# A 2048-token mixer on one core: first weights of the 64-channel unit centered on TensorE, and a new order of loads and steps

## The chip, the cores and the metric

One NeuronCore of a Trainium2 chip runs the whole program. The metric is the time of one execution on the device in microseconds, as the median of several runs. The profile is that of one execution. In it PE is TensorE's matmuls, PEld its weight loads, DVE is VectorE, ACT ScalarE, POOL GpSimd, and SP the engine that issues most DMAs.

## What is computed

For 2048 tokens x of 448 channels, the result is `g * a + (1 - g) * b`, with a sigmoid gate g per token. Branch a is a state-space convolution, which the kernel replaces by running sums wherever a check on the parameters allows. Branch b is what this case is about:

```python
h  = gelu(layernorm(x) @ w1)                     # 448 -> 448
hs = concat(h[:, 0:112] shifted +1 token, h[:, 112:224] shifted -1,
            h[:, 224:336] shifted +2, h[:, 336:448] shifted -2) @ w2
x1 = x + hs
b  = x1 + gelu(layernorm(x1) @ w3) @ w4          # 448 -> 1792 -> 448
```

## The kernel before

Tokens go in four blocks of 512, and each block runs two layers. A "unit" is a tile of at most 128 hidden channels: per block four units of the mixing layer (groups 0, 2, 1, 3 in this order, so unit numbers 0, 1, 2, 3 of block 0 and 4, 5 of block 1 are groups 0, 2, 1, 3 and 0, 2), then 14 units of the second layer. Group 2 has only 64 channels of its own; this is the "64-channel unit" (unit number 1). Each unit takes a first product (x times w1, function `first`), a GELU on ScalarE, and a second product into four accumulators (`second`).

Products are made in split precision. Each operand is cut into a high part and a low part, by a ScalarE copy into the reduced type and a VectorE subtraction, and high x high, low x high and high x low are summed. The 448 rows of x stand in four chunks of 128 partitions (index k); the last chunk has only 64 rows, and its upper half holds the low part.

The mean of the layer norm is taken out of the weights: w1 loses its column means before the split ("centering"), so that x need not be centered. The means come from TensorE: a matmul whose stationary operand is a column of 1/448 repeated 128 times (`cm`) leaves in each of the 128 rows of a PSUM bank the column means of w1; VectorE then subtracts them (`center`). These matmuls are full fp32, two instructions each; the products use the reduced type, one instruction each.

All of the first 35 us is issued in an order written by hand, the string ORDER (L1090). Each word is one step, and steps of an engine run in the order of the string:

- `w` a warming matmul; `m0` to `m3` the column means of group 0 to 3 (L912, L927, L863); `wt`, `ws` VectorE sums of chunks, so that m2 and m0 need fewer matmuls; `c0` to `c3` centering on VectorE (L935); `h0` to `h3` the high part on ScalarE and `l0` to `l3` the low part on VectorE of a group's first weights; `wh`, `wl` the same for its second weights
- `xha`, `xhb`, `xla`, `xlb` high and low parts of the left and right half of x's first block; `xh1`, `xl1` of the second block
- `p1:h2a` a first product of unit 1 with the high weights, chunk 2 (x in place of h: low part of x; l: low weights), on the left half a, on b, or on all 512 tokens; `s0:12` a second product of unit 0
- `sa`, `sb` token statistics, `ra0` nine small VectorE steps to 1/sqrt(variance), `ra`, `rm`, `rn` its rows, turned by TensorE; `xz`, `pe`, `sk` the first tokens of the shifted groups: `pe` (L839) multiplies the centered weights of groups 1 and 3 by two tokens
- `mu`, `hd`, `cp`, `tl` scaling, GELU, high and low part of a unit's hidden values

The loads of this stage are issued in `first_loads` (L255), most by SP and three by ScalarE. A DMA waits for the completion slot of an earlier one before it is issued. The names used below: u0a, u0b (two halves of group 0's w1), u1, u2, u3 (w1 of the other groups), xa, xb, xc (left half of x's first block, chunks 0-1 and 2-3, and its right half), t0 to t5 tokens for the statistics, v0, v1 the second weights, n1 the next block, id the identity matrix. In this order two steps of ScalarE's queue stand ahead of its first arithmetic, and SP issues xa first.

Of the kernel before, what the change touches and what calls it, by code (L numbers as in the profile page):

```python
# [179 lines left out]
def mixer_and_small_steps(ctx, tc, xs, gg, okm, x, xT, xb, x0, w1, w2, w3, w4, gate, par, logdt, dskip, ident, out):  # L180
# [74 lines left out]
    def first_loads():  # L255

        r = raw[0] = room([128, 4 * XW], "raw")
        parts0.append(r[:, :4 * HW].rearrange("p (k t) -> p k t", k=4))
# [7 lines left out]
        load_w1(act, 2)
        sp(r[:, :2 * HW], x0[:, :2 * HW])
        act(w1r[:, :256], w1[:, :256])  # L268
        sp(w1r[:, 256:512], w1[:, 256:512])
        act(xs[:, 0, :], x[0:128])  # L270
        sp(r[:, 2 * HW:4 * HW], x0[:, 2 * HW:4 * HW])
        load_w1(sp, 1)
        load_x(1, 2)
        load_x(2, 3)
        load_w1(sp, 3)
        load_x(3, 5)
        sp(r[:, 4 * HW:], x0[:, 4 * HW:])
        sp(idt, ident)
        sp(w2r[:, 0], w2[:, 0])  # L279
        load_xt(1)  # L280
        sp(w2r[:, 1:4], w2[:, 1:4])
        load_x(NT + 1, 2 * NT + 1)
# [621 lines left out]

    WS = {}

    def presum():

        WS[1] = big.tile([128, 128], F32, name="ws", tag="lt")
        nc.vector.tensor_add(WS[1], W1R[0][:, 0, :], W1R[0][:, 1, :])  # L910

    def presum_mean():  # L912
        a, p = W1R[0], mean_bank(0)
        for q, (c, r) in enumerate(((1, a[:, 3, :]), (0, a[:, 2, :]), (0, WS[1]))):
            nc.tensor.matmul(p, cm[:, c:c + 1].to_broadcast([128, 128]), r, start=q == 0, stop=q == 2)

    def presum_unit2():

        a = W1R[2]
        v = big.tile([128, GD], F32, name="ws", tag="yt")  # L920
        WS[0] = v
        nc.vector.tensor_add(v, a[:, 0, :], a[:, 1, :])
        yield
        nc.vector.tensor_add(v, v, a[:, 2, :])
        yield

    def unit2_mean():  # L927

        p = mean_bank(2)
        for q, c in enumerate((1, 0)):  # L930
            nc.tensor.matmul(p, cm[:, c:c + 1].to_broadcast([128, 128]), WS[0] if q else W1R[2][:, 3, :],
                             start=q == 0, stop=q == 1)
            yield
# [160 lines left out]
    p2:l2a p0:h0b p3:h2a xlb p2:h0a sa1 p1:h1b p2:x2a p3:h3a p2:h1b sb3 p0:h2b xlb p0:l0b sa2 p2:h0b p1:x0b
    xlb p3:x1b p0:x2b,h1b l3 p0:l1b p2:x0b wh0 p1:x2b p0:x0b p1:h3b ra0 p0:x1b ra0 p0:h3b p2:x2b ra0 p3:h1b
    xh1 p3:l3a ra0 p3:x2b p2:l0a ra0 p2:l0b ra0 xh1 p1:h0b p3:h2b ra0 p3:l2b p2:x1b ra0 p0:l3b xh1 ra0
    p2:h3b p1:x1b sk p1:h2b wl0 p0:l2b xh1 p3:l1a ra sk uf0 sk p2:l2b xl1 rm p2:l1a p3:x0b uf1 p3:l0b mu0
    p3:x0a sk p4:l1 mu0 p4:h1 sk ad1 p2:h2b hd0 p3:l3b,h0b p4:h3 hd0 mu0 p3:l2a mu1 p2:l1b bm p2:l3a mu1
    p3:h3b hd0 p3:x1a,h1a,l1b hd0 p4:l2 xl1 s0:00 hd0 s0:10 p5:h3 xl1 hd0 p4:x0 s0:01 ba p5:h0 sb7 s0:20 hd0
    hd1 p2:l3b tl0 s0:21 p3:l0a p5:x1 sb7 wh2 mu2 s0:30 p5:x0 cp1 p4:h2 sb5 p3:h0a s0:02 wh1 p4:h0 tl0 s0:11  # L1100
    sb5 s0:31 tl1 hd2 s0:22 p5:h2 p4:l3 wl2 hd2 p5:h1 hd2 s0:12 sb7 p4:x1 cp2 s1:11,31 sb5 s1:20 cp2 s1:01
    sb7 s0:32 sb5 s2:30 tl2 s1:30,10 s2:20 ra1 mu3 s2:00 s1:21 s2:22 ra1 s1:00 wl1 hd3 p4:l0 s2:10 ra1 wh3
    s2:02 ra1 s2:01 ra1 s2:31 hd3 xl1 hd3 s2:11,32,21 ra1 cp3 s2:12 ra1 p4:x2 ra1 wl3 p5:x2 s3:30 uf5 s3:20
# [198 lines left out]
```

## Time and profile before

| | before |
|---|---|
| median of 3 runs | 371.17 us (371.15 to 371.31) |
| the profiled execution, first to last instruction | 368.9 us |
| TensorE busy | 363.4 us (99%) |
| VectorE / ScalarE / GpSimd busy | 84% / 59% / 17% |

The page gives busy time of each engine, the chain of work that ended last, and the costliest groups of instructions. A line of a timeline is: start, duration, engine, source line, operation, output and inputs, shape, count of merged instructions. Matmuls overlap at their ends, so the distance between two starts is what one costs, and its duration is longer.

### The profile page before, as it was taken

The page shows a single profiled execution, that of the slowest core. Times are in us where ns is not written, and L with a number is a line of the kernel's source. Part 1 is how long each engine was busy: PE and PEld are TensorE (multiplying, and loading weights), DVE is VectorE, ACT ScalarE, POOL GpSimd, SP SyncE. Part 2 cuts the span into 40 slices and gives each one's busy share as a digit, 9 for nine tenths or more (in the row PEclk, how much of TensorE's full clock was granted, in tenths as well). Part 3 has the DMA queues.
Part 4 walks back from the last instruction along what each step waited for, and adds up shares of the span by engine and source line. Part 5 has one row for each costly group of instructions (what it writes and reads, how often), then busy time and mean ns, then how long its engine had stood idle before and what let it go on. Part 6 is the DMA issues. An engine that isn't in the chain of part 4 may idle for free.

```text
span 368.9 us, 5308 instructions
## 1 busy us (share of the span) xinstructions
PE 363.4 (99%) x1734; PEld 314.3 (85%) x1734; DVE 308.1 (84%) x571; ACT 215.9 (59%) x383; POOL 63.3 (17%) x176
## 2 busy tenths in 40 slices
PE   8999999999999999999999999999999999999995
PEld 4988888888888888888888888888888888888885
DVE  4999979797999997378799899998789999998533
ACT  5987668777684637944274774554756645455220
POOL 1000432000300000110013433224243234000000
PEclk9999999999999999999999999999999999999999
DMA  7994116626948064001833514457385611361213
GB/s 258 393 398 157 38 65 124 134 88 251 390 134 203 0 116 156 0 0 52 178 107 77 89 28 94 114 165 131 83 131 121 179 16 28 79 179 30 64 50 105
DMA packets 88479, 46.14 MB, mean 125 GB/s; under 512 B 67200, under 2 KB 82944, under 8 KB 87808
## 3 DMA queue, kind: packets, MB, share of 16 engines
q1 hardware_dynamic: 88016, 45.27, 45.6%
q10 hardware_dynamic: 432, 0.49, 0.4%
q8 instruction: 15, 0.25, 0.3%
q14 instruction: 16, 0.13, 0.1%
HBM read 34.74 MB, written 11.01 MB: 124 GB/s over the span
## 4 chain that ended last, share of the span: by engine, by line
PE 93%; DMA 4%; ACT 1%; DVE 0%; ACTq 0%; SPq 0%; issue 0%
PE p L478 46%; PE acc L603 45%; DMA raw<-xb_in 2%; DMA xs<-x_in 2%; PE acc L638 1%; ACT xh L394 1%; PE p L638 0%; PE misc L363 0%; DVE xh L401 0%; ACT uf L996 0%; ACTq L268 0%; DVE uf L1007 0%; SPq L279 0%; ACT ug L1020 0%; ACT ug L1023 0%
## 5 line engine op out<-in xcount | busy, mean ns | idle before, releaser
L539 ACT ACTIVATE uf<-p 128x512 f32<-128x512 f32 x56 | 33.4, 597 | 113.3 <-PE p L478 113.2
L478 PE MATMUL p<-xh,w3l 128*128 128x512 f32 x224 | 70.1, 394 | 0.0
L478 PE MATMUL p<-xh,w3h 128*128 128x512 f32 x224 | 70.1, 394 | 0.0
L758 DVE TENSOR_TENSOR_SCAN z<-z,carry 128x512 f32<-128x512 f32 x48 | 61.5, 1282 | 4.2 <-POOL z L752 0.5
L603 PE MATMUL acc<-w4l,uh 128*128 128x448 f32 x216 | 56.3, 367 | 0.0
L603 PE MATMUL acc<-w4h,uh 128*128 128x448 f32 x216 | 56.0, 365 | 0.0
L603 PE MATMUL acc<-w4h,ul 128*128 128x448 f32 x216 | 55.8, 364 | 0.0
L569 DVE TENSOR_TENSOR ul<-uf,uh 128x512 fp32r<-128x512 f32 x56 | 38.1, 681 | 20.1 <-ACT uh L549 20.0
L478 PEld LDWEIGHTS p<-xh,w3l 128*128 128x128 f32 x224 | 42.1, 188 | 9.8
L478 PE MATMUL p<-xl,w3h 128*128 128x512 f32 x168 | 47.7, 392 | 0.0
L478 PEld LDWEIGHTS p<-xh,w3h 128*128 128x128 f32 x224 | 42.1, 188 | 6.6
L603 PEld LDWEIGHTS acc<-w4h,uh 128*128 128x128 f32 x216 | 40.5, 188 | 6.0
L603 PEld LDWEIGHTS acc<-w4h,ul 128*128 128x128 f32 x216 | 40.6, 188 | 3.5
L603 PEld LDWEIGHTS acc<-w4l,uh 128*128 128x128 f32 x216 | 40.6, 188 | 3.4
L753 ACT ACTIVATE z<-zs,nu 128x512 f32<-128x512 f32 x64 | 42.3, 710 | 0.6 <-DMA zs<-xT_in 0.6
L478 PEld LDWEIGHTS p<-xl,w3h 128*128 128x128 f32 x168 | 31.5, 188 | 7.2
L549 ACT ACTIVATE uh<-uf 128x512 fp32r<-128x512 f32 x56 | 35.4, 633 | 1.8
L752 POOL COPY z<-carry 128x1 f32<-128x1 f32 x48 | 32.1, 679 | 16.0 <-DVE zs L764 15.9
L760 POOL COPY carry<-z 128x1 f32<-128x1 f32 x48 | 13.1, 273 | 105.7 <-DVE z L758 105.0
L344 POOL TENSOR_TENSOR t<-r 128x4 f32<-128x4 f32 (+1 forms) x5 | 3.1, 627 | 117.4 <-DVE r L343 117.4
L603 PE MATMUL acc<-w2l,uh 128*128 128x448 f32 x64 | 19.9, 368 | 0.0
L758 DVE TENSOR_TENSOR_SCAN z<-z,carry,zero 128x512 f32<-128x512 f32 x16 | 19.9, 1247 | 0.0
(207 smaller groups left out, 541.8 us busy)
## 6 DMA issues: line engine op xcount, KB each, us to landing
zs<-xT_in SPq DMA_DIRECT2D x4, 1024.0 KB, 8.3
yd<-yt SPq DMA_DIRECT2D x56, 64.0 KB, 2.0
ysb<-yd SPq DMA_DIRECT2D x16, 224.0 KB, 2.7
raw<-xb_in SPq DMA_DIRECT2D x3, 1032.0 KB, 12.6
raw<-w_in SPq DMA_DIRECT2D x3, 1024.0 KB, 5.6
xd<-xt SPq DMA_DIRECT2D x16, 192.0 KB, 2.1
xr<-xd SPq DMA_DIRECT2D x16, 192.0 KB, 3.1
raw<-w_in SPq DMA_DIRECT2D x3, 896.0 KB, 4.6
```

Source lines behind the costliest of these rows:

```text
L344: eng.tensor_mul(t, y, y)
L394: nc.scalar.activation(XH["a", b][:, k, :], raw[b][:, k, :], AF.Copy)
L478: nc.tensor.matmul(p[:, t0:t1], (wl if w else wh)[:, k, :], (xl if x_ else xh)[:, k, o + t0:o + t1], start=(q == 0 and fresh), stop=stop i ...
L539: nc.scalar.activation(UF[n], P1[n], AF.Gelu_apprx_tanh)
L549: nc.scalar.activation(UH[n], UF[n], AF.Copy)
L569: nc.vector.tensor_sub(UL[n], uf, f32(UH[n]))
L603: nc.tensor.matmul(ACC[j], (UL if p == 2 else UH)[n][:, t], wl if p == 1 else wh, start=first_, stop=last_)
L638: nc.tensor.matmul(acc, (UL if p == 2 else UH)[m][:, t], (wl if p == 1 else wh)[:, c], start=q == last and m == n and p == 0, stop=m > n a ...
L752: nc.gpsimd.tensor_copy(z4[:, m, 0:1], carry[:, k, m:m + 1])
L753: nc.scalar.activation(z4[:, m, 1:], ZS[b][:, k, :], AF.Copy, scale=nu[:, k, m:m + 1])
L758: nc.vector.tensor_tensor_scan(z, z, up, carry[:, k, m:m + 1], OP.add, OP.add)
L760: nc.gpsimd.tensor_copy(carry[:, k, m:m + 1], z[:, TB - 1:])
```

## The change

The 64-channel unit: its four chunks (4 x 64 columns) are no longer summed on VectorE and centered there. TensorE computes the centered weights in PSUM: four full-precision matmuls put minus the mean into all 256 columns, and a fifth, with the identity matrix, adds the weights. The split into high and low part reads PSUM. Group 0's means take four matmuls, with no sum on VectorE. Groups 1 and 3 get their means in one accumulation of four matmuls of 256 columns (`mean_ops(1, 3)`). The first block of x lies in DRAM as three contiguous pieces. The loads follow a list: first all of w1 and the tokens t0, then the identity matrix, then x. The order of steps is a new one.

```diff
-    cm = big.tile([128, 2], F32, name="cm")
+    cm = big.tile([128, 4], F32, name="cm")
...
+        def x0_part(q):
+            w = (2 * HW, 2 * HW, 4 * (XW - HW))
+            return x0[sum(w[:q]) * 128:sum(w[:q + 1]) * 128].rearrange("(p t) -> p t", p=128)
...
+        for word in LOADS.split():
+            queue, _, job = word.partition(":")
+            jobs[job](act if queue == "act" else sp)
...
+        for c, s in ((2, -1.0), (0, 1.0)):
+            nc.gpsimd.memset(cm[:, c:c + 1], s / D)
+            nc.gpsimd.memset(cm[:64, c + 1:c + 2], s / D)
+            nc.gpsimd.memset(cm[64:, c + 1:c + 2], 0.0)
...
-        pm[g] = ps.tile([128, GD if g == 2 else 128], F32, name="pm", tag=("misc", "acc2", "acc1", "acc3")[g], bufs=1)
-        return pm[g]
+    def mean_bank(gs):
+        g = gs[0]
+        p = ps.tile([128, len(gs), GD if g == 2 else 128], F32, name="pm", tag=("misc", "acc1", "acc2")[g], bufs=1)
+        for q, g in enumerate(gs):
+            pm[g] = p[:, q, :]
+        return p
...
+    def mean_ops(*gs):
+        p = mean_bank(gs)
         for k in range(4):
             c = int(k == 3)
-            nc.tensor.matmul(p, cm[:, c:c + 1].to_broadcast([128, 128]), W1R[g][:, k, :], start=k == 0, stop=k == 3)
+            w = W1R[gs[0]] if len(gs) == 1 else w1r[:, W1O[1]:].rearrange("p (i k m) -> p k i m", i=2, k=4)
+            nc.tensor.matmul(p, cm[:, c:c + 1].to_broadcast([128, 128]), w[:, k], start=k == 0, stop=k == 3)
+            yield
+
+    def centered_ops(g):
+        w = W1R[g]
+        p = pm[g] = ps.tile(list(w.shape), F32, name="pm", tag=("misc", "acc1", "acc2")[g], bufs=1)
+        for k in range(4):
+            c = 2 + int(k == 3)
+            nc.tensor.matmul(p, cm[:, c:c + 1].to_broadcast([128, 128]), w[:, k:k + 1, :].to_broadcast(list(w.shape)),
+                             start=k == 0, stop=False)
+            yield
+        nc.tensor.matmul(p, idt, w, start=False, stop=True)
+        yield
...
-            return w1d[:, k0:k1, :GD], w1d[:, k0:k1, GD:], W1R[g][:, k0:k1]
+            return w1d[:, k0:k1, :GD], w1d[:, k0:k1, GD:], pm[g][:, k0:k1]
...
-    TASKS.update(wt=presum_unit2(), m2=unit2_mean(), c2=each((center, 2, 0, 2), (center, 2, 2, 4)),
+    TASKS.update(m0=mean_ops(0), m1=mean_ops(1, 3), m2=centered_ops(2),
...
+    LOADS = """
+    sp:u0b sp:u2 act:u0a act:t0 sp:u1 sp:u3 act:id sp:xa sp:xb sp:xc sp:t1 sp:t3 sp:t2 sp:n1 sp:v1 sp:v0 sp:t5
+    """
+
...
-    w w wt xha w wt m2 w xla m2 ws c2 m0 c2 h2 h2 l2 l2 p1:h0a c0 xha xz p1:x0a sk w xz sa0 xla p1:h2a m1 c0
-    h0 xla sa1 l0 p0:x0a p1:x1a p0:h0a c1 p1:x2a h0 p1:h1a,h3a sa0 ld m3 l0 h1 p0:h3a c3 p0:x2a,l2a,l1a sa2
...
+    w sa0 w w m0 xz m0 m0 m0 c0 h0 m2 c0 h0 sa0 m2 m2 sk m2 w m2 h2 h2 w xha l0 l0 m1 m1 m1 l2 l2 m1 c3 p1:h1a
+    p0:l1a c1 xla p1:h0a p0:h0a xz p0:l0a,h1a xha xla xla pe p1:h2a p0:h2a ld p0:l2a h1 p2:h1a h3 p0:x0a,x1a l1
+    p2:h2a p1:x1a p2:h0a p1:x2a p2:x2a xhb xhb p0:h3a,h0b p1:x0a p0:l0b p2:h1b p0:l3a p1:h3a sa1 p1:h2b
...
```

## Rows read from the trace of the kernel before

**Rows 1.** The page: span, and busy time, share and instructions by engine.
```profile
span 368.9 us, 5308 instructions
...
PE 363.4 (99%) x1734; PEld 314.3 (85%) x1734; DVE 308.1 (84%) x571; ACT 215.9 (59%) x383; POOL 63.3 (17%) x176
```
**Rows 2.** The chain in order of time: start us, us, what.
```profile
21.02 0.67 PE acc L603 x2
...
360.04 3.68 PE acc L638 x18
```
**Rows 3.** Stretches: us, busy PE, PEld, DVE, ACT, POOL (count); clock, DMA, GB/s.
```profile
0.00:4.56 4.56, 3.62 (x10) 1.27 (x11) 0.11 (x1) 1.83 (x3) 0.90 (x15) 1.00 0.54 165
4.56:10.57 6.01, 5.24 (x37) 4.41 (x38) 4.96 (x15) 4.21 (x13) 0.45 (x3) 1.00 1.04 360
...
21.02:34.20 13.18, 13.18 (x66) 11.67 (x67) 12.83 (x34) 9.51 (x23) 0.00 (x0) 1.00 0.78 285
...
10.86:28.58 17.72, 17.64 (x122) 16.05 (x121) 17.15 (x48) 14.39 (x34) 0.90 (x4) 1.00 1.02 394
```
**Rows 4.** Timeline of PE up to 35 us.
```profile
0.77 3.62 PE L903 MATMUL pw<-const-bfloat16-1.0 128*128 128x512 bf16 x10 [0.77 <-PEq L1294]
4.56 0.41 PE L931 MATMUL pm<-w1r,cm 128*128 128x64 f32 x2 [0.17 <-DMA w1r<-w_in]
4.80 0.38 PE L903 MATMUL pw<-const-bfloat16-1.0 128*128 128x512 bf16 x1
...
5.26 0.66 PE L915 MATMUL pm<-w1r,cm 128*128 128x128 f32 x4
...
6.71 0.39 PE L478 MATMUL p<-xh,w1d 128*128 128x256 f32 x1 [0.38 <-DVE w1d L943]
...
7.85 0.39 PE L478 MATMUL p<-xh,w1d 128*128 128x256 f32 x1 [0.40 <-ACT xh L956]
8.07 1.05 PE L867 MATMUL pm<-w1r,cm 128*128 128x128 f32 x8
...
9.08 0.28 PE L478 MATMUL p<-xl,w1d 128*128 128x256 f32 x1
...
9.67 1.15 PE L867 MATMUL pm<-w1r,cm 128*128 128x128 f32 x8
10.57 0.36 PE L478 MATMUL p<-xh,w1h 128*128 128x256 f32 x1
...
20.43 0.52 PE L478 MATMUL p<-xh,w1l 128*128 128x256 f32 x2
...
21.53 0.39 PE L478 MATMUL p<-xh,w1d 128*128 128x512 f32 x1
...
34.15 0.85 PE L478 MATMUL p<-xh,w1h 128*128 128x512 f32 x3
```
**Rows 5.** Two lines' matmuls: ns min/median/max, first and last start.
```profile
L867 PE MATMUL pm<-w1r,cm x16: 272/275/363, 8.1 to 10.5; 128*128 128x128 f32 x16
...
L845 PE MATMUL pe<-w1r,xz x8: 191/193/194, 12.2 to 12.4; 128*2 128x32 f32 x8
```
**Rows 6.** Timeline of DVE: c3, the step after it, and wl1.
```profile
10.86 0.69 DVE L937 TENSOR_TENSOR w1r<-w1r,pm 128x512 f32<-128x512 f32 x1 [0.42 <-PE pm L867]
11.46 0.62 DVE L974 BATCH_NORM_STATS2 b<-xs 128x6 f32<-128x448 f32 x1
...
28.58 0.62 DVE L943 TENSOR_TENSOR w2l<-w2r,w2h 128x448 fp32r<-128x448 f32 x1
```
**Rows 7.** SP's own waits, 0 to 20 us: total, times, longest.
```profile
SPq L246 <- DMA w1r<-w_in: 1.4, 1, 1.4
SPq L278 <- DMA xs<-x_in: 0.9, 1, 0.9
```
**Rows 8.** Line L267 (xa): from issue to landing.
```profile
DMA to landing us min/median/max: 3.5/3.5/3.5
```
**Rows 9.** Line L264 (u2 by ACT; u1, u3 by SP): from issue to landing.
```profile
DMA to landing us min/median/max: 3.7/4.8/5.7
```

More of the change, by code (lines that the diff above doesn't have):

```diff
@@ L264, in load_w1, with load_to @@
             queue(w1r[:, t], w1[:, t])
[L266 to L282, printed above, removed]
+        def load_to(queue, j0, j1):
+            queue(xs[:, j0:j1, :], x[j0 * 128:j1 * 128].rearrange("(j p) d -> p j d", p=128))
+        jobs = dict(
+            u2=lambda q: load_w1(q, 2), u1=lambda q: load_w1(q, 1), u3=lambda q: load_w1(q, 3),
+            u0a=lambda q: q(w1r[:, :256], w1[:, :256]), u0b=lambda q: q(w1r[:, 256:512], w1[:, 256:512]),
+            xa=lambda q: q(r[:, :2 * HW], x0_part(0)), xb=lambda q: q(r[:, 2 * HW:4 * HW], x0_part(1)),
+            xc=lambda q: q(r[:, 4 * HW:], x0_part(2)),
+            t0=lambda q: load_to(q, 0, 1), t1=lambda q: load_to(q, 1, 2), t2=lambda q: load_to(q, 2, 3),
+            t3=lambda q: load_to(q, 3, 5), t5=lambda q: load_to(q, NT + 1, 2 * NT + 1),
+            id=lambda q: q(idt, ident), v0=lambda q: q(w2r[:, 0], w2[:, 0]), v1=lambda q: q(w2r[:, 1:4], w2[:, 1:4]),
+            n1=lambda q: load_xt(1))
+        for word in LOADS.split():
+            queue, _, job = word.partition(":")
+            jobs[job](act if queue == "act" else sp)
     def constants():
-        nc.gpsimd.memset(cm[:, 0:1], 1.0 / D)
-        nc.gpsimd.memset(cm[:64, 1:2], 1.0 / D)
-        nc.gpsimd.memset(cm[64:, 1:2], 0.0)
+        for c, s in ((2, -1.0), (0, 1.0)):
+            nc.gpsimd.memset(cm[:, c:c + 1], s / D)
+            nc.gpsimd.memset(cm[:64, c + 1:c + 2], s / D)
+            nc.gpsimd.memset(cm[64:, c + 1:c + 2], 0.0)
         nc.gpsimd.memset(one, 1.0)
@@ L903, in warm_up @@
             nc.tensor.matmul(pw, warm[:, 0:128], warm, start=True, stop=True)
[L905 to L933, printed above, removed]
     def center(g, k0=0, k1=4):
@@ L1051, in mixer_and_small_steps @@
     TASKS = dict(
-        ws=each((presum,)), m0=each((presum_mean,)), w=each(*((warm_up, 1) for _ in range(5))),
+        w=each(*((warm_up, 1) for _ in range(5))),
         xha=each((x_hi, 0, lh), (x_hi, 2, lh)), xhb=each((x_hi, 0, rh), (x_hi, 2, rh)),
@@ L1073, in mixer_and_small_steps @@
         if g:
-            TASKS[f"m{g}"] = each((col_means, g))
             TASKS[f"c{g}"] = each((center, g))
@@ L1094, in mixer_and_small_steps @@
[L1094 to L1103, printed above, removed]
@@ new lines, in mixer_and_small_steps @@
+    sb3 p2:l0a l3 sb3 sa2 sb3 sa2 p2:l2a p1:x0b p3:x1a,h3a p2:x0a xlb p0:h3b p1:h3b p3:l2b uf1 xh1 p0:l2b,l3b
+    uf0 p2:x2b,h3b,l3a p3:h0b sb3 ra0 ra0 ra0 p3:l0b ra0 p2:x1b ra0 ra0 p2:l1b ra0 p3:l3a ra0 p2:h2b ra0 p3:h2b
+    p2:l1a p3:h1a ad1 sk ra mu0 mu0 rm mu1 p3:l1b p2:l3b,l2b xh1 xh1 p5:h0 mu1 p4:h0 p3:l3b p4:l0 mu0 xh1 p4:h1
+    p3:x1b hd0 wh0 xl1 xl1 hd0 wl0 hd0 hd0 ba hd0 hd1 p3:l2a,h0a p4:h2 sk xl1 p5:h1 p2:x1a,l0b hd0 p3:x0b hd0
+    xl1 p3:h2a p5:h3 s0:10 p3:x2b sb5 p3:x0a p4:x0,l1 bm p3:x2a tl0 p3:l0a,l1a tl0 p4:x1 mu2 p5:x0 cp1 sb5 p5:x1
@@ new lines, in mixer_and_small_steps @@
+    wh1 s0:00 tl1 p4:l3 wh2 hd2 p3:h3b p4:h3,l2 p5:x2,h2 s0:22 wl2 sk sk s0:32 sb7 s0:01,31 sk s1:00 hd2 s0:11
+    hd2 cp2 s0:21 s1:01 p4:x2 s1:20 s0:12 s1:11 mu3 sb7 s1:21 s0:30,02 s1:10 s0:20 s1:31 tl2 s2:32,30,22 hd3 wh3
+    sb7 sb5 s2:10 sb7 s2:02 sb5 wl1 cp2 ra1 s2:12 hd3 hd3 cp3 s1:30 s2:31 ra1 wl3 s2:21,00 ra1 cp3 s2:20 s3:20
+    s2:01 ra1 uf5 ra1 s3:00 ra1 s3:21 ra1 s3:11 s2:11 ra1 ra1 rn tl3 s3:01 sb9 s3:32,31,12,10 sb9 bn mu4 hd4 hd4
+    s3:02 re re s3:22 re ad5 s3:30 hd4 cp4 tl4 cp4 re mu5 hd5 cp5
@@ L1278 @@
         x=x, xT=xT, xb=np.stack([xT[:, :, b * TB:b * TB + XW] for b in range(1, NB)]),
-        x0=np.concatenate([xT[:, :, t].reshape(128, -1) for t in (slice(0, HW), slice(HW, XW))], axis=1),
+        x0=np.concatenate([xT[:, k, t].ravel() for k, t in ((slice(0, 2), slice(0, HW)), (slice(2, 4), slice(0, HW)),
+                                                            (slice(0, 4), slice(HW, XW)))]),
         w1=np.concatenate([ktile(a["B_w1"][:, c]).reshape(128, -1) for c in (rows[0], rows[2], rows[1], rows[3])],
```

7 lines of the change are left out of this document (1 added, 6 removed).

## The prediction

> **What bounds the kernel now.** I read the page's engine totals first, then the chain that ended last, then busy time by stretch, then TensorE's own order at the start. The totals show TensorE busy for 99% of a span of 368.9 us [rows 1]. The chain shows where that becomes the limit: from 21.02 us on every piece is a TensorE piece, down to the last products at 360.04 [rows 2]. The stretches agree: 5.24 of 6.01 us busy from 4.56 to 10.57, then 13.18 of 13.18 from 21.02 [rows 3]. The granted clock is 1.00 in all of them, the 2.4 GHz level. So the kernel's time is the time at which TensorE has issued the product work, and an edit of the first stage is worth exactly what it moves that work, provided nothing starves later. The median of the runs, 371.17, is 2.27 above the span; the sum is made on the span and 2.27 put back. About 0.2% (0.74 us) is the least that a measurement of this kernel can tell from no change.
>
> **A ledger for the first stage.** I measure both versions by a "product start": the moment at which TensorE would begin if its products ran back to back and all else lay ahead of them. Before: seven plus three warming matmuls run from 0.77; the last starts at 4.39 - 0.38 = 4.01 and streams 0.22 (the pitch from the `w` at 4.80 to the next start at 5.02), so TensorE is free at 4.23. Then come m2 at 4.56, a `w`, m0 at 5.26, a wait to 6.71 for the first unit's weight parts, another wait to 7.85, m1 at 8.07, m3 at 9.67, and products without a gap from 10.57 [rows 4]. Nine half-width products were issued between these, 9 x 0.12 = 1.07 us (0.12 is the pitch of the products around 9.08). Product start before: 10.57 - 1.07 = **9.50 us**.
>
> **After, step by step.** The order is now w, w, w, m0 (4 matmuls), m2 (5 of 256 columns, with one `w` inside), `w`, m1 (4 of 256 columns), products. I walk it with the durations of before.
> - m0: each full-precision matmul is two instructions. Eight of 128 columns took 1.05 us from 8.07, that is (1.05 - 0.275)/7 = 0.111 each [rows 4, 5]. Four matmuls, no VectorE pre-sum: 8 x 0.111 = 0.89. Before it was six.
> - A 256-column instruction of this kind does not occur before. Bounds: 0.119, the pitch of a 256-column product, if a column costs the same; 0.222, twice the 128-column pitch, if it costs double. The rows decide for the second: 32 columns took 193 ns and 128 took 275, that is 0.85 ns per column [rows 5], while products of 256 and 512 columns took 0.28 and 0.39, 0.43 ns per column [rows 4]. I take 0.222.
> - The Trainium skill ("TensorE: Matmul & The Clock Gate", section Back-to-back issue gap) gives 262 cycles for 256 columns with no surcharge, an estimate of 0.109 us; its page "Perfetto Trace Analysis" (section Engine Utilization) halves the output rate for the full-precision pair. By the first, m2 and m1 together would cost 2.0 us, by the second 4.0. The 0.85 against 0.43 ns sides with the second.
> - m2: 10 x 0.222 = 2.22, where before it was four short ones, some 0.5 in all (two took 0.41 from 4.56). m1 with both units: 8 x 0.222 = 1.78, the same columns as m1 and m3 before (1.78); joining them saves nothing by itself. The two warming matmuls within: 0.44.
> - Start: TensorE is free at 4.23 as before, for the same ten warming matmuls precede it. The first load on each queue is now one half of unit 0's weights (128 KB). The first SP load of before, 260 KB, landed after 3.5 us [rows 8] and the first ACT one after 3.7 [rows 9], so 4.2 to 4.45. With fewer bytes beside it I take 4.25.
> - Sum: 4.25 + 0.89 + 1.78 + 0.22 + 0.44 + 0.22 + 1.78 = **9.58 us**. The removed waits (0.33, 0.64, 0.57 and some tenths) are eaten by the added full-precision work: 4.9 us of it, where before had 3.0 (0.5 + 0.7 + 1.8).
>
> **The new wait.** After m1, TensorE has six products (h and l of chunks 0 and 1, 0.71 us) and then `pe`, which reads the weights of units 1 and 3 after centering. Both centerings now wait for one accumulation: m1's last instruction ends at 9.36 + 0.38 = 9.74, c3 runs, then c1. The two VectorE steps of this shape start 0.60 apart and last 0.69 [rows 6], so c1 ends at about 11.05. TensorE stands at `pe` from 10.29: **0.80 us** lost. Before, m1 and m3 had banks of their own, c1 was done before m3 was, and other products covered c3. Behind `pe` queue all products; h1 and the three x residuals (ACT and VectorE) are queued behind c1 too, but by the walk they come just in time (h1 at 11.7 for its product at 11.8).
>
> **VectorE later.** From c3 at 10.86 to the residual of unit 1's second weights at 28.58 VectorE is busy for 17.15 of 17.72 us [rows 3, 6]. In the new order c3 starts 1.1 us earlier (9.78), but c1 (0.60), three x residuals (1.4, estimated from the 0.69 of 512 columns: one as wide, two half as wide that don't overlap) and one more residual of the next block (0.6) are moved behind it and two small steps of 0.2 ahead. The same residual so starts at 9.78 + 17.7 + 2.2 = 29.7, less at most 0.57 of idle time, and ends at 29.8 to 30.3, when TensorE by my walk wants it at 30.3. Shorter waits of 0.05 to 0.2 lie on the way. I book 0.5, with bounds 0.1 and 0.9. On the other side before lost about 0.35 when its first second-layer product waited for its input (the product before it started by 20.55 and streams 0.12, the next runs from 21.02) [rows 2, 4]; in the new order that input is ready ahead of its turn.
>
> **Loads.** Program order shares the completion slots: the ninth load waited 1.4 us for the first one and the thirteenth 0.9 us for the fifth [rows 7]. In the new order xb (ninth) waits for u0b, xc for u2, and so on, so xb is issued at 4.2 and not at 2.6. Queue ahead of it hides this: 1,444 KB lie before it, and 752 KB had moved by 4.56 (165 GB/s x 4.56), the rest at 360 GB/s [rows 3], which is 6.5. u3 is the fourth SP load with 1,184 KB up to its end; the fourth of before, with 1,384 KB, landed after 4.8 or 5.7 us, between 6.9 and 7.8 [rows 9], and m1 wants it at 7.81: free, but with 0 to 0.9 us to spare. The first x piece lands near 7.5, a us after its bytes have moved as the others did; ScalarE wants it at 8.3, when it has split unit 2's weights after m2, and the second piece at 8.9: free, with about a us each, and even later x would first fill the wait at `pe`. Contiguous x pieces keep the same 2,080-byte rows in SBUF; I cost them at nothing, 0.1 either way. The mean of unit 2 needs no subtraction any more: two VectorE steps and two pre-sums (0.9 us of VectorE) go, but they lay in a stretch where VectorE idled, worth nothing beyond the waits already counted.
>
> **Sum.** Product start +0.08, wait at `pe` +0.80, later VectorE waits +0.5, wait of before gone -0.35: +1.03 us. Span 368.9 + 1.0 = 369.9, time 371.17 + 1.03 = **372.2 us** (+0.28%). After 34 us the same steady work follows: by the same walk the next second-layer inputs are ready between 36.6 and 37.3, as TensorE comes to them from 37.7 on. So the microsecond stays to the end.
>
> **Rivals.**
> - *Full-precision columns at the single rate.* m2 and m1 take 0.119 each instruction, 1.85 us less. Then TensorE would wait for the first x piece instead (0.4) and for c1 (0.4) where it now waits 0.8, and the end comes at about -0.8 against before: 370.4, faster. For it: only that the weight load of 128 columns paces a 128-column pair as well. Against: the 0.85 ns per column. 9%.
> - *The order hides what I count as waits.* If VectorE keeps its gaps of before, and a product or two more is issued ahead of `pe` in effect because x comes late, the cost is +0.08 + 0.3 to 0.8 - 0.35: 371.2 to 371.7, no difference that can be told. For it: both waits rest on margins of tenths. 28%.
> - *The reorder pays.* The new order has no loss after the product start beyond 0.2 and VectorE catches up: 9.58 + 0.2 against 9.50 + 0.35, and the next tenths of idle time before the steady part go too: 370.9; and down to 370.3 where the small gaps of before between 10.57 and 34.15 are fewer too, half of the chance. 13%.
> - *Weights land late.* u3 behind u0, u2, t0 and u1 lands at 8.8 in place of 6.9 to 7.8; m1 waits a us with nothing else in the queue: 373.2. It decides from 7.8 us on. 10%.
>
> **How the numbers follow.** The forecast, 372.2 with a range of its own from 371.7 to 372.7, has 40%. Slower by over 0.2% (above 371.9) holds about three quarters of the forecast, the late weights and a part of the second rival: 0.48. Same: the rest of the forecast, most of the second rival, half of the third: 0.36. Faster (below 370.4): 0.16. The range from 370.3 to 373.0 takes in the first rival and all but the late weights.
>
> **What would show it.** Right, if the changed profile has ten m2 instructions of 256 columns about 0.22 apart, products starting near 9.6 and a TensorE gap of 0.6 to 1.0 us in front of the eight `pe` instructions, released by a VectorE centering. Wrong, if the m2 instructions stand 0.12 apart, if the gap stands before m1 (weights) or before the first product (x), or if TensorE goes through `pe` without waiting. TensorE's last first-block product of the second layer should end near 35.2, against 34.15 before [rows 4]; if it ends before 34.15 the ledger is wrong.

## The result and the profile after

| | before | after |
|---|---|---|
| median, same chip | 371.31 us (371.15 to 372.04, 5 runs) | 372.91 us (372.31 to 373.32, 5 runs) |
| ratio after to before | | 1.0043, interval 1.0032 to 1.0054 |
| the profiled execution: span | 368.9 us | 371.5 us (its time: 373.24) |
| first steady product of the second layer | 34.15 us | 36.10 us |

The change made the kernel slower by 0.43%, 1.60 us. The forecast was slower by 1.03 us, 372.2; the measured 372.91 lies just above the range that the forecast gave itself (371.7 to 372.7) and inside the wide one (370.3 to 373.0). A second set of runs of the same two kernels, told below, gives 372.57 against 371.06, 1.51 us.

First the totals on the page of after: span, then busy time, share and instructions by engine.

```profile
span 371.5 us, 5309 instructions
...
PE 365.6 (98%) x1734; PEld 316.0 (85%) x1734; DVE 307.6 (83%) x566; ACT 216.0 (58%) x383; POOL 64.9 (17%) x179
```

Against [rows 1] TensorE is busy for 2.2 us more, while VectorE has lost only 0.5. The number of TensorE instructions is the same: a few long ones stand where short ones stood. Next TensorE's timeline of after up to the first steady product (start us, us, engine, line, operation, tiles, shape, count, idle time before and its releaser).

```profile
0.77 4.42 PE L922 MATMUL pw<-const-bfloat16-1.0 128*128 128x512 bf16 x10 [0.77 <-PEq L1286]
4.99 1.44 PE L874 MATMUL pm<-w1r,cm 128*128 128x128 f32 x8
6.27 1.89 PE L882 MATMUL pm<-w1r,cm 128*128 128x256 f32 x8
...
8.21 0.59 PE L885 MATMUL pm<-w1r,idt 128*128 128x256 f32 x2
...
8.86 1.89 PE L874 MATMUL pm<-w1r,cm 128*128 128x256 f32 x8
10.40 0.47 PE L481 MATMUL p<-xh,w1d 128*128 128x256 f32 x1
10.71 0.28 PE L481 MATMUL p<-xh,w1l 128*128 128x256 f32 x1
...
11.18 0.29 PE L481 MATMUL p<-xh,w1h 128*128 128x256 f32 x1
12.22 0.39 PE L851 MATMUL pe<-w1r,xz 128*2 128x32 f32 x8 [0.75 <-DVE w1r L926]
...
36.10 0.85 PE L481 MATMUL p<-xh,w1h 128*128 128x512 f32 x3
```

Read against [rows 4]: the two waits of before in front of its first products, at 6.71 and 7.85, are gone. From 0.77 to 11.18 TensorE issues without a stop. In their place stand ten full-precision instructions of 256 columns for m2 (with the two `w` beside them 8.86 - 6.27 = 2.59 us) and one new wait, in front of `pe`. VectorE's two centerings, which `pe` waits for, on VectorE's timeline of after (same columns):

```profile
10.79 1.29 DVE L926 TENSOR_TENSOR w1r<-w1r,pm 128x512 f32<-128x512 f32 x2 [0.98 <-PE pm L874]
```

VectorE had idled for 0.98 us until m1 was done; c3 and c1 then run back to back and end at 12.08, and `pe` starts at 12.22. The stretches of after (us, busy PE, PEld, DVE, ACT, POOL with counts, granted clock, DMA share, GB/s) show where it stood idle:

```profile
4.99:10.62 5.63, 5.63 (x30) 4.92 (x29) 2.01 (x6) 3.01 (x10) 0.45 (x3) 1.00 1.03 381
10.62:22.90 12.28, 11.53 (x95) 10.98 (x94) 11.48 (x30) 9.76 (x23) 0.19 (x2) 1.00 1.03 402
22.90:36.10 13.20, 13.16 (x67) 11.38 (x66) 12.78 (x37) 9.29 (x24) 1.27 (x2) 1.00 0.62 231
```

TensorE lacks 0.75 us in the middle stretch, all of it the wait at `pe`, and 0.04 in the last. A delay shorter than the overlap of two matmuls is not idle time in these columns; it shows only in the distance between two starts, and the section on the prediction reads the later waits that way.

**Where the time went.** By the ledger of the prediction, the product start of after is one pitch (0.12) ahead of its second product, 10.71 - 0.12 = 10.59, against 9.50 before: +1.09. From there to the first steady product it takes 36.10 - 10.59 = 25.51, against 34.15 - 9.50 = 24.65: +0.86. Together +1.95 in these two executions. The second figure repeats (24.65 and 24.64 in b0 and b1, 25.50 to 25.52 in e0, e1 and e6, all below); the first does not. From the first steady product to the end of the span the two kernels do the same work. TensorE's part of it, up to the end of its last matmul, takes 331.05 to 331.12 us in all twelve profiles; the rest, 3.6 to 4.4 us with the last output writes, makes the spread. The whole takes 334.7 to 335.0 us in the three profiles of before's order and 334.7 to 335.5, on average 0.3 more, in the nine others. Whether that is chance, three profiles against nine don't show.

### The profile page after: what moved, and what is told of

Read it like the earlier page. It is cut to its first block, busy times and chain, and to the rows that moved or that the text cites. A ratio compares the mean times of both kernels' runs of the same rounds, so it can differ in the third digit from the quotient of the medians.

```text
span 371.5 us, 5309 instructions
## 1 busy us (share of the span) xinstructions
PE 365.6 (98%) x1734; PEld 316.0 (85%) x1734; DVE 307.6 (83%) x566; ACT 216.0 (58%) x383; POOL 64.9 (17%) x179
## 4 chain that ended last, share of the span: by engine, by line
PE 98%; DVE 0%; issue 0%; DVEq 0%
PE p L481 48%; PE acc L606 45%; PE pw L922 1%; PE acc L641 1%; PE pm L874 1%; PE misc L366 0%; PE pm L882 0%; PE p L641 0%; DVE w1r L926 0%; PE pm L885 0%; PE pe L851 0%; DVE xs L630 0%; PE misc L738 0%; DVEq L952 0%
## 5 line engine op out<-in xcount | busy, mean ns | idle before, releaser
L542 ACT ACTIVATE uf<-p 128x512 f32<-128x512 f32 x56 | 33.5, 598 | 112.5 <-PE p L481 112.4
L606 PE MATMUL acc<-w2h,uh 128*128 128x448 f32 x64 | 20.1, 367 | 0.0
```

What stands on the lines that cost most here:

```text
L542: nc.scalar.activation(UF[n], P1[n], AF.Gelu_apprx_tanh)
L606: nc.tensor.matmul(ACC[j], (UL if p == 2 else UH)[n][:, t], wl if p == 1 else wh, start=first_, stop=last_)
```

## The experiments

Every experiment is read in two ways: its median against before on the same chip, and three marks of its profiled execution: m0's first start (for the kernels made from before, that of m2), the first product's row, and the first steady product. Medians of single kernels scatter by tenths, so the marks carry the detail.

| kernel | median us (runs) | ratio to before, interval | m0 | first product | steady | last two differ by |
|---|---|---|---|---|---|---|
| after | 372.91 (5) | 1.0043 [1.0032, 1.0054] | 4.99 | 10.40 | 36.10 | 25.70 |
| e0_after | 372.57 (6) | 1.0048 [1.0031, 1.0065] | 4.48 | 9.50 | 35.19 | 25.69 |
| e1_warm4 | 372.09 (10) | 1.0025 [1.0016, 1.0035] | 3.75 | 9.94 | 35.65 | 25.71 |
| e2_fill | 372.34 (6) | 1.0039 [1.0025, 1.0054] | 4.99 | 10.08 | 35.05 | 24.97 |
| e3_dve2 | 371.48 (12) | 1.0007 [0.9994, 1.0021] | 4.53 | 8.66 | 34.35 | 25.69 |
| e4_split | 372.52 (9) | 1.0038 [1.0025, 1.0052] | 4.99 | 11.04 | 36.09 | 25.05 |
| e6_oldx | 372.73 (6) | 1.0044 [1.0027, 1.0061] | 4.66 | 9.68 | 35.38 | 25.70 |
| e5_all | 370.91 (12) | 0.9997 [0.9983, 1.0011] | 3.92 | 9.31 | 34.40 | 25.09 |
| e7_loads | 371.42 (12) | 1.0013 [1.0002, 1.0023] | 3.75 | 8.86 | 34.81 | 25.95 |
| b0_before | 371.30 (8) | 0.9998 [0.9986, 1.0011] | (4.66) | | 34.61 | |
| b1_warm4 | 371.27 (11) | 1.0002 [0.9992, 1.0011] | (4.44) | | 34.32 | |

The runs of before beside them had medians of 371.06 (e0 to e3), 371.17 (e4 to e6 and b1) and 371.23 (e7 and b0).

### The changed kernel once more (e0_after)

No edit.

> The changed kernel once more, nothing altered. Theory (the start of the granted full clock falls at a different moment in each execution; in the profile of before the warming matmuls sped up at 3.3 us, in that of the changed kernel at 5.6 us): the median stays 1.1 to 1.7 us above before, the runs spread over about 1 us, and in this profile the first mean of group 0 starts anywhere between 4.2 and 5.1 us, right at the end of the ten warming matmuls. Rival (the late start belongs to the change, its weights land late): it starts near 5.0 again and a load ends the wait before it.

Its TensorE timeline:

```profile
0.77 3.87 PE L922 MATMUL pw<-const-bfloat16-1.0 128*128 128x512 bf16 x10 [0.77 <-PEq L1286]
4.48 1.05 PE L874 MATMUL pm<-w1r,cm 128*128 128x128 f32 x8
...
9.50 0.47 PE L481 MATMUL p<-xh,w1d 128*128 128x256 f32 x1
9.81 0.28 PE L481 MATMUL p<-xh,w1l 128*128 128x256 f32 x1
...
11.32 0.39 PE L851 MATMUL pe<-w1r,xz 128*2 128x32 f32 x8 [0.75 <-DVE w1r L926]
...
35.19 0.85 PE L481 MATMUL p<-xh,w1h 128*128 128x512 f32 x3
```

The same program has its steady products 0.91 us earlier than in the first profile. All of that lies ahead of the first product: the ten warming matmuls take 3.87 and not 4.42, m0's eight instructions 1.05 and not 1.44, and from the first product to the steady one the two executions differ by 0.01. As the theory had it, m0 starts where the warming matmuls end and waits for no load; the six runs spread over 1.85 us, though, and not over about 1. In this execution (371.83 us) the ledger gives a product start of 9.81 - 0.12 = 9.69 and a steady product 1.04 after that of before. That this is the forecast of +1.03 is in part luck, for both lie at the low end of their scatter: this one has the shortest time of its six (median 372.57), and the profiled one of before has a span of 368.9 where the 21 executions of before beside e0 have a median of 369.3. Against the second profile of before (b0, below) the same difference is 35.19 - 34.61 = 0.58.

### The centering of the 64-channel unit back on VectorE (e3_dve2)

```diff
...
-            return w1d[:, k0:k1, :GD], w1d[:, k0:k1, GD:], pm[g][:, k0:k1]
+            return w1d[:, k0:k1, :GD], w1d[:, k0:k1, GD:], W1R[g][:, k0:k1]
...
-    TASKS.update(m0=mean_ops(0), m1=mean_ops(1, 3), m2=centered_ops(2),
+    TASKS.update(m0=mean_ops(0), m1=mean_ops(1, 3), m2=unit2_mean(), wt=presum_unit2(), c2=each((center, 2, 0, 2), (center, 2, 2, 4)),
...
-    w sa0 w w m0 xz m0 m0 m0 c0 h0 m2 c0 h0 sa0 m2 m2 sk m2 w m2 h2 h2 w xha l0 l0 m1 m1 m1 l2 l2 m1 c3 p1:h1a
+    w sa0 w w wt wt m0 xz m0 m0 m0 c0 h0 m2 c0 h0 m2 sa0 c2 c2 sk w h2 h2 w xha l0 l0 m1 m1 m1 l2 l2 m1 c3 p1:h1a
```

Here `unit2_mean` is the two short matmuls of before, `presum_unit2` its two VectorE sums, and the split reads the centered weights from SBUF again.

> The changed kernel with the 64-channel unit's means and centering as before (two VectorE sums, two short means, centering on VectorE), at the same place in the order. Theory (the five 256-column matmuls cost 2.2 us and the two short ones 0.5): the means of groups 1 and 3 start about 1.6 us sooner unless their weights hold them (they landed at 7.3 us in the profile of the changed kernel), and the median falls by 1.0 to 1.6 us. Rival (the time of x's landing, 8.1 to 8.8 us, and the gap ahead of pe hide it): under 0.5 us.

Its TensorE timeline:

```profile
4.53 1.05 PE L874 MATMUL pm<-w1r,cm 128*128 128x128 f32 x8
5.41 0.33 PE L890 MATMUL pm<-w1r,cm 128*128 128x64 f32 x2
...
5.81 0.60 PE L939 MATMUL pw<-const-bfloat16-1.0 128*128 128x512 bf16 x2
7.05 1.97 PE L874 MATMUL pm<-w1r,cm 128*128 128x256 f32 x8 [0.65 <-DMA w1r<-w_in]
...
10.48 0.39 PE L851 MATMUL pe<-w1r,xz 128*2 128x32 f32 x8 [0.76 <-DVE w1r L943]
```

1.09 us of the median comes back (372.57 to 371.48, same chip), within the 1.0 to 1.6 expected (the intervals of e0 and e3 don't meet), and 0.84 of the mark (35.19 to 34.35). m2 takes 0.40 here (5.81 less 5.41) in place of some 2.2. Only part of the difference is gained, because TensorE now arrives early: m1 stands for 0.65 us on the weights of groups 1 and 3, which land at 7.05. The gap at `pe` is the same. So **the largest single part of what the change costs is the 64-channel unit's centering on TensorE**; how much of it taking it back can win is bounded by a load.

### The gap at `pe` filled (e2_fill), and the merged means taken apart (e4_split)

e2 puts the second high part and two of the three low parts of x's left half ahead of c3 and c1, and nine more first products ahead of `pe`:

```diff
-    w sa0 w w m0 xz m0 m0 m0 c0 h0 m2 c0 h0 sa0 m2 m2 sk m2 w m2 h2 h2 w xha l0 l0 m1 m1 m1 l2 l2 m1 c3 p1:h1a
-    p0:l1a c1 xla p1:h0a p0:h0a xz p0:l0a,h1a xha xla xla pe p1:h2a p0:h2a ld p0:l2a h1 p2:h1a h3 p0:x0a,x1a l1
...
+    w sa0 w w m0 xz m0 m0 m0 c0 h0 m2 c0 h0 sa0 m2 m2 sk m2 w m2 h2 h2 w xha l0 l0 m1 m1 m1 l2 l2 m1 xha xla xla c3 p1:h1a
+    p0:l1a c1 p1:h0a p0:h0a xz p0:l0a,h1a xhb xhb xla p1:h2a p0:h2a ld p0:l2a,x0a,x1a p1:x1a,x2a p0:x2a p1:x0a pe
+    h1 p2:h1a h3 p2:h2a l1 p2:h0a p2:x2a p0:h3a,h0b,l0b p2:h1b p0:l3a p1:h3a sa1 p1:h2b
...
```

> The changed kernel with other work in the gap ahead of pe: two x residuals ahead of the two centerings on VectorE, the right half's high parts ahead of h1 on ScalarE, and nine more products ahead of pe. Theory (TensorE really loses the 0.8 to 0.9 us there): the gap ahead of pe falls under 0.3 us and the median falls by 0.6 to 0.9 us against the changed kernel. Rival (VectorE is the bound up to 33 us, so that what pe gains is waited for later): less than 0.3 us.

e4 leaves the order and gives groups 1 and 3 a bank and an accumulation each, with c1 between them:

```diff
...
-    TASKS.update(m0=mean_ops(0), m1=mean_ops(1, 3), m2=centered_ops(2),
+    TASKS.update(m0=mean_ops(0), m1=mean_ops(1), m3=mean_ops(3), m2=centered_ops(2),
...
-    w sa0 w w m0 xz m0 m0 m0 c0 h0 m2 c0 h0 sa0 m2 m2 sk m2 w m2 h2 h2 w xha l0 l0 m1 m1 m1 l2 l2 m1 c3 p1:h1a
-    p0:l1a c1 xla p1:h0a p0:h0a xz p0:l0a,h1a xha xla xla pe p1:h2a p0:h2a ld p0:l2a h1 p2:h1a h3 p0:x0a,x1a l1
+    w sa0 w w m0 xz m0 m0 m0 c0 h0 m2 c0 h0 sa0 m2 m2 sk m2 w m2 h2 h2 w xha l0 l0 m1 m1 m1 l2 l2 m1 c1 m3 m3 m3 m3 c3 p1:h1a
+    p0:l1a xla p1:h0a p0:h0a xz p0:l0a,h1a xha xla xla pe p1:h2a p0:h2a ld p0:l2a h1 p2:h1a h3 p0:x0a,x1a l1
```

> The changed kernel with the means of groups 1 and 3 in two accumulations of four 128-column matmuls each, in banks of their own, c1 issued between them. Theory (c1 waits for group 3's share of the joint accumulation, and pe for both centerings): c1 starts about 0.9 us sooner, the gap ahead of pe falls from 0.9 to 0.3 us, and the stretch from the first product to the end of the hand-ordered stage from 25.5 to 24.9 us. Rival (VectorE's later work is the bound): the gap shrinks and that stretch stays within 0.2 us of 25.5.

TensorE's timeline of e2_fill around `pe`:

```profile
11.96 0.28 PE L481 MATMUL p<-xl,w1d 128*128 128x256 f32 x1
12.17 0.39 PE L851 MATMUL pe<-w1r,xz 128*2 128x32 f32 x8
```

and of e4_split:

```profile
9.34 1.95 PE L874 MATMUL pm<-w1r,cm 128*128 128x128 f32 x16
11.04 0.36 PE L481 MATMUL p<-xh,w1d 128*128 128x256 f32 x1
11.24 0.28 PE L481 MATMUL p<-xh,w1l 128*128 128x256 f32 x1
...
12.15 0.39 PE L851 MATMUL pe<-w1r,xz 128*2 128x32 f32 x8 [0.16 <-DVE w1r L926]
```

Both take the wait away, by different means: e2 by work ahead of it, which leaves 0.09 us (from 11.96 + 0.12 to 12.17), e4 by an earlier c1, which leaves 0.32 (from 11.71 + 0.12 to 12.15). In after it is 0.92. From the first product to the second it takes 0.31 us behind a 256-column instruction (after) and 0.20 behind one of 128 columns (e4), so the way to the first steady product is counted here from the product start of the ledger, one pitch ahead of the second product: 25.51 in after, 35.05 - 10.27 = 24.78 in e2, 36.09 - 11.12 = 24.97 in e4. Of the 0.83 that e2 takes away 0.73 comes back, and of the 0.60 of e4 0.54. So the wait is real loss, it comes from centering two groups after one accumulation, and nearly all of it is kept to the steady part. The medians don't show it: 372.34 and 372.52 against 372.57 are not clear of the scatter, and the 0.6 to 0.9 that e2 was to take off the median did not come. The two profiled executions say why it can be hidden: m0 started at 4.99 in both and took 0.96 (e2, to 5.95) and 1.71 us (e4, to 6.70), against 4.48 and 0.89 in e0. A term that has nothing to do with the edit is as large as the edit.

### Three warming matmuls fewer, in after and in before (e1_warm4, b1_warm4)

```diff
-        warm_up(7)
+        warm_up(4)
```

> The changed kernel with four warming matmuls ahead of the order in place of seven, so seven and not ten before the first mean. In the changed kernel's profile both halves of group 0's weights had landed at 3.5 us, and TensorE came to them at 4.99, when the warming matmuls were through. Theory (the warming matmuls hold up the first mean): it starts 0.6 us (early clock) to 1.3 us (late clock) sooner, and the median falls by 0.6 to 1.2 us against the changed kernel. Rival (the warming matmuls bring the full clock, fewer of them put it off): no gain, or a loss of up to 0.6 us.

> The kernel before with four warming matmuls ahead of the order in place of seven. Theory (there a load, landing at 4.4 us, starts the first mean, so that the warming matmuls matter only where the clock rises late): the median stays within 0.3 us of before, and its slowest runs are nearer to its fastest. Rival (the warming matmuls cost before as much as the changed kernel): 0.4 to 0.7 us faster.

TensorE's timeline of e1_warm4, made from after:

```profile
0.77 3.14 PE L922 MATMUL pw<-const-bfloat16-1.0 128*128 128x512 bf16 x7 [0.77 <-PEq L1286]
3.75 2.05 PE L874 MATMUL pm<-w1r,cm 128*128 128x128 f32 x8
```

and of b1_warm4, made from before:

```profile
4.44 0.66 PE L931 MATMUL pm<-w1r,cm 128*128 128x64 f32 x2 [0.52 <-DMA w1r<-w_in]
...
7.48 0.65 PE L903 MATMUL pw<-const-bfloat16-1.0 128*128 128x512 bf16 x1
7.86 0.58 PE L478 MATMUL p<-xh,w1d 128*128 128x256 f32 x1
8.24 1.16 PE L867 MATMUL pm<-w1r,cm 128*128 128x128 f32 x8
```

In after TensorE takes m0 straight away, at 3.75, and the median falls by 0.48 (372.57 to 372.09), less than the 0.6 to 1.2 expected. The interval of e1 touches those of the single sets of the changed kernel, but its median lies below all of them (372.91, 372.57, and 372.73 for e6, whose order is the same). Its one profile doesn't show the gain: m0's row lasts 2.05 us against 1.05 in e0, and the first product comes at 9.94 against 9.50. So whether fewer warming matmuls put the full pace off, as the rival has it, stays open. In before the first matmul stands 0.52 us on its load, and the median stays, as the theory had it: ratio 1.0002. The first weights of after land 2.7 to 2.8 us after an issue at 0.7, so that the ten warming matmuls hold m0 up, to 4.99 in after and to 4.48 in e0.

The same lines show the term that scatters. The median `w` lasted 631 ns in after and 520 in before (one line's instructions in each, durations ns min/median/max, first and last start). In after:

```profile
L922 PE MATMUL pw<-const-bfloat16-1.0 x12: 379/631/631, 0.8 to 8.6; 128*128 128x512 bf16 x12
```

In before:

```profile
L903 PE MATMUL pw<-const-bfloat16-1.0 x12: 379/520/634, 0.8 to 7.1; 128*128 128x512 bf16 x12
```

An execution begins with matmuls at half their later pace (512 columns in 0.42 us, later 0.22) and at some moment changes to the full one. The moment can be counted from the rows. In before's profile the first ten starts span 3.24 us, which makes about six pitches of 0.42 and three of 0.22 and puts it at 3.4 us; in e0 it lies at 3.9; in after at 5.8, for all ten were slow (9 x 0.42 = 3.79) and half of m0; in e4 at 6.7, behind all of m0; in b1 at about 8.4, since the product at 7.86 still lasts 0.58 us (0.39 for the same one in before) and of m1's eight only the first is slow (1.16 us for the row, against 1.05). The granted clock reads 1.00 in every window of these stretches, the 2.4 GHz level, so that column does not show it; the two paces are in the ratio of the 1.2 and the 2.4 GHz level, but no row here names the cause. Ahead of it TensorE ran without a stop in after, e0 and e4; in b1 it had been idle for 0.52 us at least once. A change at 8.4 us in place of 3.4 cost b1 next to nothing: steady products at 34.32 against 34.15. In before the slow matmuls stand beside waits for loads and for ScalarE and VectorE; in after they stand in a chain with no wait, and each slow microsecond costs half of one. Five profiles show it, whose TensorE work up to the products is the same (e4 has its 256 columns of m1 in two halves):

| profile | change of pace, us | product start, us |
|---|---|---|
| e0_after | 3.9 | 9.69 |
| e6_oldx | 4.3 | 9.86 |
| e2_fill | 5.1 | 10.27 |
| after | 5.8 | 10.59 |
| e4_split | 6.7 | 11.12 |

Over 2.8 us of the one the other moves by 1.43, and its mean is 10.31. In before's order it does not follow: 9.50 with a change at 3.4, 9.96 at 4.3 (b0), 9.68 at 8.4 (b1).

### The old layout of x (e6_oldx)

```diff
...
-            w = (2 * HW, 2 * HW, 4 * (XW - HW))
-            return x0[sum(w[:q]) * 128:sum(w[:q + 1]) * 128].rearrange("(p t) -> p t", p=128)
+            w = (0, 2 * HW, 4 * HW, 4 * XW)
+            return x0[:, w[q]:w[q + 1]]
...
```

> The changed kernel with the first block of x laid out in DRAM as before, its three pieces read as strided rows. Theory (the pieces have rows of 2,080 bytes in SBUF either way, and nothing waits for them): x lands within 0.3 us of the changed kernel's 8.1 and 8.8 us and the time is within 0.3 us of the changed kernel. Rival (contiguous pieces land sooner and the order rests on it): the first x piece lands a us or more later and the first product waits for it.

372.73 us, and 25.70 from first product to steady, as in after. The two left pieces land 5.6 and 5.1 us after their issue, against 5.5 and 5.4 in after, that is within 0.1 us of the same moments, as the theory had it. Three contiguous pieces are worth nothing that these runs can tell.

### All three remedies (e5_all), and the weights ahead of everything (e7_loads)

e5 is e1, e2 and e3 together. e7 changes its loads too, and moves the token statistics `sa0` behind the first products, since t0 comes later:

```diff
-    sp:u0b sp:u2 act:u0a act:t0 sp:u1 sp:u3 act:id sp:xa sp:xb sp:xc sp:t1 sp:t3 sp:t2 sp:n1 sp:v1 sp:v0 sp:t5
+    sp:u0b sp:u1 act:u0a act:u2 sp:u3 sp:xa act:xb sp:xc sp:t0 sp:t1 sp:t3 sp:id sp:t2 sp:n1 sp:v1 sp:v0 sp:t5
```

> Three edits at once in the changed kernel: four warming matmuls ahead of the order, the filled gap ahead of pe, the 64-channel unit centered on VectorE. Theory (the three prices add, but the means of groups 1 and 3 can't start before their weights, which landed near 7.0 us): they start at 7.0 as with the VectorE centering alone, the stage ends 0.6 to 0.9 us sooner than there (33.5 to 33.8 us), the median is 370.5 to 370.9, and the runs spread less, since a load and not the clock sets the start. Rival (VectorE takes the gain back once it has more to do): no more than 0.3 us below the VectorE centering alone, so 371.2 or more.

> The three edits together (fewer warming matmuls, filled gap, 64-channel unit on VectorE) plus another order of loads: all of w1, then x, and the tokens t0 and the identity matrix after them; ScalarE's first statistics moved behind the loads they need. Theory (with the three edits the stage is bound by the weights of groups 1 and 3, on which TensorE waited 1.8 us until 7.7): they land near 6.2, x near 7.5, the stage ends between 33.0 and 33.6 us against 34.15 before, and the median is 370.0 to 370.5. Rival (x is the next bound, or VectorE, which then gets its whole list no sooner): the stage ends after 34.0 us and the median is not under 370.7.

TensorE's timeline of e5_all:

```profile
3.92 1.13 PE L874 MATMUL pm<-w1r,cm 128*128 128x128 f32 x8
...
7.70 1.96 PE L874 MATMUL pm<-w1r,cm 128*128 128x256 f32 x8 [1.83 <-DMA w1r<-w_in]
```

and TensorE's waits of e7_loads up to 40 us (for what: total, times, longest):

```profile
PE pm L874 <- DMA w1r<-w_in: 0.7, 1, 0.7
PE pe L851 <- DVE w1r L943: 0.3, 1, 0.3
PE misc L366 <- DVE r L336: 0.3, 1, 0.3
PE p L481 <- ACT w1h L946: 0.2, 1, 0.2
```

e5 takes 1.7 us off e0's time (370.91) and so gives back all that the change cost, but it isn't faster than before (interval 0.9983 to 1.0011): TensorE is free at 5.87 and stands 1.83 us on the weights of groups 1 and 3. The prices did not add as its theory had it: m1 started at 7.70 and not at 7.0, the first steady product came at 34.40 and not between 33.5 and 33.8, and the runs did not draw together (370.33 to 372.67). Its interval overlaps that of e3, so it is not shown to be faster than the VectorE centering alone. e7 was to win that time and did not. The wait falls to 0.7 and the first product comes at 8.86, but from there it takes 25.95 us: `pe` waits for VectorE again, a product waits for ScalarE, and the displaced statistics are late at L366. Its theory (a first steady product at 33.0 to 33.6, 370.0 to 370.5 us) missed with 34.81 and 371.42; the rival, that VectorE and x take the gain back, held. No version here is clearly faster than before.

### The kernel before once more (b0_before)

No edit.

> The kernel before once more, nothing altered, for a second profile of it. Theory (before starts its first mean when a load lands, at 4.4 us, and its waits cover a late clock): whatever the clock's moment is, the stage ends at 34.0 to 34.4 us. Rival (the first profile of before was only a lucky one): with a late clock it ends up to a us later. And the stretch from the stage's end to the last instruction, 334.7 us in the profile of before and 334.8 to 335.5 in those of the changed kernel and its variants: 334.7 again if the last writes differ by program, anything between if they differ by execution.

TensorE's wait for the second piece of x in b0, ScalarE's step that ends it, and the same step in before:

```profile
8.29 0.38 PE L478 MATMUL p<-xh,w1d 128*128 128x256 f32 x1 [0.78 <-ACT xh L956]
```
```profile
7.61 0.64 ACT L956 ACTIVATE xh<-raw 128x520 fp32r<-128x520 f32 x1 [1.01 <-DMA raw<-x_in]
```
```profile
7.16 0.64 ACT L956 ACTIVATE xh<-raw 128x520 fp32r<-128x520 f32 x1 [0.63 <-DMA raw<-x_in]
```

371.30 us, ratio 0.9998. Its steady products start at 34.61, above the 34.0 to 34.4 of the theory. The change of pace is not the cause: m0 starts at 5.29 against 5.26 in before. The 0.46 us arise where ScalarE waits for a load: the second piece of x comes 0.45 us later than in before, and TensorE's product at 7.85 [rows 4] stands at 8.29 here. So before's start moves by some tenths of a microsecond from execution to execution too, by the landing of a load, and a difference of that size between two single profiles says nothing. 0.91 between two profiles of after is twice that. From the stage's end to the last instruction it is 335.0 us here against 334.7 in the first profile, so that stretch differs by execution.

## Why the prediction was right, and where its size was off

**Price of the full-precision columns: right.** Eight m2 instructions in after lie (1.89 - 0.38) / 7 = 0.216 us apart; forecast 0.222. This excludes the rival of the single rate (0.119) and its 370.4. The Trainium skill's "TensorE: Matmul & The Clock Gate", section Back-to-back issue gap, would have made it 0.109, an estimate from its 262 cycles; the halved rate of its "Perfetto Trace Analysis", section Engine Utilization, agrees with the 0.216 if it is taken for each of the two instructions. The price per column does not hold for narrow ones: in before two instructions of 64 columns took 0.24 us from 4.56 to 4.80 [rows 4], 0.12 each, and those of 128 columns 0.111. No run here shows what sets that least distance. The work from m0 to the product start was forecast at 9.58 - 4.25 = 5.33; e0 took 9.69 - 4.48 = 5.21.

**The wait at `pe`: right.** From 11.18 + 0.12 = 11.30 to 12.22 it is 0.92 us (forecast 0.80), released by VectorE's centering. 0.09 of it stands between a product and `pe` without a wait too (e2), so the loss is 0.83. e2 and e4 show that 0.73 and 0.54 come back when it is removed in whole and in part, in two different ways.

**Later waits and before's lost wait: right, though one row was misread.** Forecast +0.5 and -0.35, net +0.15. Measured from the product start on is +0.86, less 0.83 at `pe`: +0.03. TensorE's idle time from 22.90 to 36.10 is only 0.04 us, but the starts show the later waits. TensorE of after, and then the VectorE step that ends the wait:

```profile
27.02 0.57 PE L606 MATMUL acc<-w2l,uh 128*128 128x448 f32 x2
27.62 0.45 PE L606 MATMUL acc<-w2h,uh 128*128 128x448 f32 x1
27.90 0.57 PE L606 MATMUL acc<-w2l,uh 128*128 128x448 f32 x2
```
```profile
26.79 0.69 DVE L570 TENSOR_TENSOR uh<-uf,uh 64x512 fp32r<-64x512 f32 x1
```

Two such matmuls stand 0.20 us apart, so the one at 27.62 was due at 27.42; it comes behind the VectorE step that ends at 27.48, and the next one 0.28 later and not 0.20. With 0.1 more at 24.32 that is near 0.4 of the 0.5, at another step than the residual of the second weights that the prediction had in mind. The 0.35 of before is there too: the product that starts by 20.55 was due to be followed 0.23 later and is followed at 21.02, and the next distance is 0.30 and not 0.20, together 0.34 [rows 2, 4]. But that product lasts 0.40 us and so has 512 columns; the prediction took it for one of 256, which streams 0.12. That its 0.35 came out is luck.

**The product start: the term that was mis-sized.** Forecast 9.58 against 9.50, +0.08. Measured 10.59 in the first profile and 9.69 in the second, and 10.31 on average in the five of the table above; before's two profiles have 9.50 and 9.96, on average 9.73. So the term is nearer to +0.58. The step that failed is "TensorE is free at 4.23 as before, for the same ten warming matmuls precede it", and behind it the assumption that m0 costs 0.89. In after's profile the ten ended at 4.99 (+0.74 on 4.25) and m0 took 6.27 - 4.99 = 1.28 (+0.39), with 0.12 back on the rest. Ten matmuls at a mixture of two paces are no constant: before's profile shows one draw of the moment at which the pace changes, 3.4 us, the earliest of those read here (up to 8.4). I read the 4.23 as a property of the ten matmuls. The other part of the fault is that a late change was next to no cost to before, whose waits cover it (b1), and is a full cost to after, which has none. The +0.58 and the +0.86 behind the product start make +1.44, where the medians moved by +1.60 and +1.51. That the scatter of this moment makes up the 0.5 us by which they exceed the forecast (+1.03) is still an inference: it shows in the profiles, but the runs that were only timed don't show their moment, and the 0.3 us at the end of the span may have a share. The 2.27 between span and time was a sign that before's profile lay at the low end: in all runs with both on record the time is 1.7 to 1.9 above the span.

**Loads: right in effect, wrong in detail.** The first halves landed earlier than I assumed. By line, from issue to landing in after:

```profile
L268 SPq DMA_DIRECT2D w1r<-w_in x3: 438/440/441, 1.2 to 2.2; - x3
DMA to landing us min/median/max: 3.4/5.2/5.3
...
L275 SPq DMA_DIRECT2D w1r<-w_in x1: 397/397/397, 0.7 to 0.7; - x1
DMA to landing us min/median/max: 2.7/2.7/2.8
```

0.7 + 2.8 = 3.5 us, where I had 4.2 to 4.45: with no warming matmuls in front the start could have been 0.75 us earlier, which e1 used in part. u3 landed near 2.2 + 5.3 = 7.5, within the 6.9 to 7.8, and hid behind m2, so the rival of late weights (373.2), whose time is the nearest to 372.91 of all, is not what happened: no matmul of after waits for a load. The completion slots cost SP less than I thought. Its waits in after:

```profile
SPq L271 <- DMA w1r<-w_in: 1.2, 1, 1.2
...
SPq L276 <- DMA w1r<-w_in: 0.3, 1, 0.3
```

An x piece (L276) waited 0.3 us for its slot (0.7 in e0) and not the 1.6 that I gave it (4.2 in place of 2.6); the 1.2 fell on tokens (L271). Against [rows 7] the longest wait is shorter by 0.2.

**The rivals.** That the order hides the waits (371.2 to 371.7) falls with the 0.75 us in front of `pe`. That the reorder pays (370.3 to 370.9) falls too: most of what it removes in waits is spent on m2 (e3: 1.09 us).
